# Another order of all engines' instructions, and operand slots turned per outward layer, in windowed attention with two gated layers

## The chip, the cores and the metric

The kernel runs on one core of a Trainium2 chip. The metric is the device time of one execution in microseconds (us), taken as the median of three runs. The engines are TensorE (PE in the rows, PEld its weight loads), VectorE (DVE), ScalarE (ACT), GpSimd (POOL) and SyncE (SP), which issues every transfer here.

## The reference

```python
# q, k, v: batch 4, heads 8, sequence 576, head size 64
scores = scale * np.matmul(q, k.transpose(0, 1, 3, 2))
mask = (rel >= 0) & (rel < window)                    # window 128
scores = np.where(mask, scores + bias[None], -1000000000.0)
attn = np.exp(scores - np.max(scores, axis=-1, keepdims=True))
attn = attn / (np.sum(attn, axis=-1, keepdims=True) + 1e-09)
x = np.matmul(attn, v)                                # -> 2304 tokens x 512
# layer 0 and layer 1, each with w_in 512 x 2048 and w_out 2048 x 512
h = x @ w_in
g = h * np.tanh(sp)                                   # layer 0, sp = softplus(h)
g = np.where(h > 0.0, h, alpha * (np.exp(np.minimum(h, 0.0)) - 1.0))   # layer 1
x = g @ w_out
```

## The kernel before

The work has five parts that follow one another. Attention runs over 4 batches, 4 head pairs and 3 row blocks each (function `unit`: scores in tile `ps_s`, a transpose in `ps_t`, values in `ps_o`, the result in `xc`). The inward product of layer 0 (`hidden`, products at L914 into `hA`, `hB`, `hC`) runs batch by batch beside the attention of the batch behind it. The outward product of layer 0 (`outward`, products at L1001 into `oA`, `oB`, `oC`), the inward product of layer 1 and the outward product of layer 1 follow, in three column chunks each. Every product of the two layers is done with seven block products instead of eight (steps P1, P5, P6, P2, P7, P3, P4). Every operand is split into two parts, a rounded copy at L529 (ACT, or L530 on DVE) and the remainder by a subtraction at L534 (DVE or POOL); three of the four part products are kept. So one step on one operand tile is six products in `hidden`, and 12 in `outward`, which I call a group. There are 56 groups in a batch of `hidden` in layer 0, and 28 in a chunk of `outward`, 84 in a layer.

Four weight sets (w = 0 to 3) arrive as 64-bit numbers in tiles `raw` and are turned into floats in `convert`: two ACT steps (L593 and L597, a few of the second on DVE), a shift on DVE (L601), an add at L604 that may stand on POOL or on DVE, and sums of blocks. Sets 1 to 3 go to DRAM and come back as tiles `w` (`load_weights`). The gate of layer 0 is the function Mish on ACT (L978), applied when the tiles `graw` are read back for the outward product; it needs another function table than the rest. So ACT loads a table when it goes from Mish to the conversions at L593 and back.

The order is made ahead by the class `Plan`. Each operation has a priority worked out backwards from due times (`rank_all`), with a shift for its group from the table `SHIFT`. `order` then plays the program through with assumed costs and emits the instructions in the order found; where an operation may stand on two engines, it chooses there. Engines run their instructions strictly in the order emitted. While PE has nothing ready in the first 90 us of that play, `order` emits unused products (L489) into it; I call them fills. No product of the kernel is placed before the time `WARM`.

On-chip tiles lie in rings of slots. A tile takes the next slot of its ring and waits until the tile before it in that slot has been read. The outward operand `hl` has its own: of the first step of layer 0, and of two steps at its end, in ring `L0`; of the first step of layer 1 in ring `L1`; all others in ring `L`, which has five slots.

```python
    wide_s, right_s = slots(wide, "w", 6, 4 * T2), slots(right, "r", 7, 4 * T2)
    plan.ring("L0", right_s[4:])
    plan.ring("L", right_s[4:] + wide_s[4:])
    plan.ring("L1", wide_s[4:])
```

The ring `L` goes on counting from layer 0 into layer 1.

Of the kernel before, what the change touches and what calls it, by code (L numbers as in the profile page):

```python
# [11 lines left out]
F32R = mybir.dt.float32r  # L12
# [9 lines left out]
AT = dict(copy=2.27, both0=-0.71, both1=-8.32, both2=-3.61, turn=0.99, held=10.7, fill=90, enough=1.5, norma=-0.5, normp=2.42,  # L22
          kappa=1.29, lag=0.9, first=-64.52, unit=2.69, h1=50.67, chunk=70.1, lead=30.24, dt=1.35, dma=-14.73,
          conv=-27.63, wadd=-0.1, soft0=0, soft1=0, soft2=0, soft3=0, eq=4, ep=2, et=6, er=3, eb=0, eraw=3, side0=1,
          side1=2, depth=4, ahead=7.48, hb=5)
SHIFT = {
# [77 lines left out]
class Plan:  # L104
# [3 lines left out]
    WARM = 6.9  # L108
# [253 lines left out]
def mm_cost(n):  # L362
    return 0.000417 * n + (0.0125 if n < 384 else 0.0153)
# [795 lines left out]
```

## Time and profile before

| | |
|---|---|
| median of 3 runs | 868.72 us (867.3 to 870.11) |
| the profiled execution: time, span | 868.03 us, 866.3 us |
| PE busy | 843.4 us, 97% of the span |
| DVE, ACT, POOL busy | 723.1, 628.3, 132.4 us |
| chain that ended last | PE 70%, DVE 12%, ACT 11%, DMA 3%, issue 3% |
| DMA | 187.67 MB, mean 217 GB/s |

The span runs from the first to the last instruction. In a row of the time line the number in brackets is how long the engine stood idle before the instruction, and who ended that. Each product group lasts some 2.1 us, so an idle time of 1 us on PE is half a group.

### The profile page before, as it was taken

The numbers are of one execution on the slowest core, as the hardware profiler recorded it, in microseconds if no ns is written. First come the engines' busy times: TensorE is split into PE (matmuls) and PEld (weight loads), VectorE is DVE, ScalarE is ACT, GpSimd is POOL, SyncE is SP. The second block draws the span as 40 slices with busy tenths as digits, with TensorE's granted clock in tenths as the row PEclk, the third lists the DMA queues.
The fourth block names the chain that finished last, engine by engine and source line by source line (L and its number), as shares of the span: only waits on it lengthen the run. The fifth ranks groups of instructions, "written<-read, shape, count | busy, mean of one in ns | idle before, by whom it ended". The sixth has DMA issues, their size and how long they took to land.

```text
span 866.3 us, 15682 instructions
## 1 busy us (share of the span) xinstructions
PE 843.4 (97%) x5403; PEld 794.1 (92%) x5403; DVE 723.1 (83%) x1590; ACT 628.3 (73%) x1421; POOL 132.4 (15%) x115
## 2 busy tenths in 40 slices
PE   9988999999999999899899999999999999999998
PEld 6767788898889999899899999989999999999998
DVE  8999998778877689799889988895978988877863
ACT  6989997677767688875897868976998944333442
POOL 0434120000003000135213043121300000000000
PEclk9999999999999999999999999999999999999999
DMA  7436667877867886674677778676778957226102
GB/s 277 138 119 214 190 211 244 280 267 258 253 225 246 286 290 235 233 254 149 232 264 258 254 249 284 218 266 214 261 253 275 313 182 229 105 96 229 41 1 73
DMA packets 85967, 187.67 MB, mean 217 GB/s; under 512 B 8576, under 2 KB 30080, under 8 KB 85888
## 3 DMA queue, kind: packets, MB, share of 16 engines
q1 hardware_dynamic: 85888, 186.68, 64.2%
q8 instruction: 42, 0.69, 0.3%
q14 instruction: 37, 0.30, 0.1%
HBM read 117.44 MB, written 69.21 MB: 215 GB/s over the span
## 4 chain that ended last, share of the span: by engine, by line
PE 70%; DVE 12%; ACT 11%; DMA 3%; issue 3%; POOL 0%; SPq 0%; DVEq 0%; ACTq 0%; POOLq 0%
PE oA L1001 19%; PE hA L914 16%; PE oC L1001 11%; PE hC L914 8%; PE hB L914 4%; PE oB L1001 4%; PE ps_o L828 3%; DMA raw<-in_w_dram 2%; PE ps_s L725 2%; DVE hl L534 2%; PE ps_t L780 2%; DVE graw L534 1%; ACT hl L529 1%; ACT p L745 1%; ACT p L760 1%
## 5 line engine op out<-in xcount | busy, mean ns | idle before, releaser
L914 PE MATMUL hA<-xt,w 128*128 128x288 f32 (+1 forms) x1344 | 232.9, 319 | 2.3 <-ACT g L529 1.7
L529 ACT ACTIVATE hl<-graw 128x768 fp32r<-128x768 f32 x161 | 134.9, 843 | 128.1 <-PE oA L1001 63.8
L1001 PE MATMUL oA<-hl,w 128*128 128x384 f32 x1152 | 215.2, 338 | 4.2 <-DVE hl L534 2.4
L914 PEld LDWEIGHTS hA<-xt,w 128*128 128x128 f32 x1344 | 209.4, 189 | 8.0 <-ACT g L529 3.7
L534 DVE TENSOR_TENSOR hl<-graw,hl 128x768 fp32r<-128x768 f32 x168 | 165.8, 996 | 52.7 <-ACT hl L529 52.3
L1001 PEld LDWEIGHTS oA<-hl,w 128*128 128x128 f32 x1152 | 202.6, 188 | 7.0 <-DVE hl L534 4.8
L914 PE MATMUL hC<-xt,w 128*128 128x288 f32 (+1 forms) x672 | 119.7, 317 | 0.2 <-DVE g L897 0.2
L1001 PE MATMUL oC<-hl,w 128*128 128x384 f32 x576 | 111.0, 343 | 4.3 <-DVE hl L534 2.4
L1001 PEld LDWEIGHTS oC<-hl,w 128*128 128x128 f32 x576 | 103.0, 190 | 6.7 <-DVE hl L534 4.1
L914 PEld LDWEIGHTS hC<-xt,w 128*128 128x128 f32 x672 | 104.6, 188 | 3.0 <-issue 1.0
L534 DVE TENSOR_TENSOR graw<-graw 128x768 f32<-128x768 f32 x96 | 92.7, 977 | 4.2 <-ACT graw L978 1.8
L604 POOL TENSOR_TENSOR bits<-bits,raw 128x512 int32<-128x512 int32 x34 | 56.1, 1655 | 254.0 <-DVE bits L601 134.7
L529 ACT ACTIVATE g<-hA 128x288 f32<-128x288 f32 (+1 forms) x144 | 61.0, 434 | 26.6 <-PE hA L914 25.3
L745 ACT ACTIVATE p<-p,st 128x128 f32<-128x128 f32 x144 | 56.4, 396 | 13.8 <-DVE st L741 13.3
L534 DVE TENSOR_TENSOR w<-w 128x512 fp32r<-128x512 f32 x84 | 59.3, 730 | 6.2 <-ACT w L529 5.6
L914 PE MATMUL hB<-xt,w 128*128 128x288 f32 (+1 forms) x336 | 60.5, 317 | 2.4 <-DVE g L897 2.1
L914 PEld LDWEIGHTS hB<-xt,w 128*128 128x128 f32 x336 | 52.5, 188 | 4.2 <-DVE g L897 2.4
L1001 PE MATMUL oB<-hl,w 128*128 128x384 f32 x288 | 54.3, 338 | 0.0
L1001 PEld LDWEIGHTS oB<-hl,w 128*128 128x128 f32 x288 | 50.9, 188 | 0.2 <-DVE hl L534 0.2
L529 ACT ACTIVATE w<-w 128x512 fp32r<-128x512 f32 x83 | 49.3, 625 | 1.2 <-DMA w<-w_in 1.0
L896 ACT ACTIVATE e<-e 128x384 f32<-128x384 f32 x96 | 49.1, 529 | 0.7
L593 ACT ACTIVATE raw<-raw 128x512 f32<-128x512 f32 x64 | 43.0, 675 | 8.0 <-DMA raw<-in_w_dram 7.5
(100 smaller groups left out, 1109.2 us busy)
## 6 DMA issues: line engine op xcount, KB each, us to landing
graw<-gate SPq DMA_DIRECT2D x96, 384.0 KB, 4.6
raw<-in_w_dram SPq DMA_DIRECT2D x64, 512.0 KB, 5.3
gate<-g SPq DMA_DIRECT2D x64, 288.0 KB, 3.6
gate<-g SPq DMA_DIRECT2D x48, 384.0 KB, 3.9
w<-w_out SPq DMA_DIRECT2D x56, 256.0 KB, 4.0
qkv<-in_qkv_dram SPq DMA_DIRECT2D x16, 512.0 KB, 4.9
w_out<-bits SPq DMA_DIRECT2D x32, 256.0 KB, 5.1
w<-w_in SPq DMA_DIRECT2D x28, 256.0 KB, 3.7
```

Source lines behind the costliest of these rows:

```text
L529: ways = [("act", act_cost(n, sbuf), lambda: nc.scalar.activation(o(), i(), AF.Copy), 0.0), ("dve", dve_cost(n, sbuf), lambda: nc.vector.t ...
L534: emit = lambda eng: eng.tensor_tensor(out=o(), in0=x(), in1=y(), op=op)
L593: act(DM, lambda raw=raw: nc.scalar.activation(raw()[:, :, 1].bitcast(F32), raw()[:, :, 1].bitcast(F32), AF.Prelu, scale=2.0 ** -112, alph ...
L604: add = lambda eng, raw=raw, bits=bits: eng.tensor_tensor(out=bits().bitcast(I32), in0=bits().bitcast(I32), in1=raw()[:, :, 0].bitcast(I32 ...
L725: nc.tensor.matmul(pss[j]()[:, n, w0:2 * P], qs()[rs, n * P:(n + 1) * P], ks()[rs, ko + w0:ko + 2 * P], start=n == 0, stop=True, skip_grou ...
L745: act(P, lambda n=n, j=j: nc.scalar.activation(prob()[:, n, j], prob()[:, n, j], AF.Exp, scale=-1.0, bias=st()[:, 0, n, j:j + 1], accum_ou ...
L760: ("act", act_cost(P, True, 1), lambda y=y, f=f: nc.scalar.activation(y(), y(), AF.Copy, scale=f()), AT["norma"]),
L780: nc.tensor.transpose(ps()[:, j], prob()[:, n, j], ident)
L828: nc.tensor.matmul(o()[j * D:(j + 1) * D, c0:c0 + math.prod(y.shape[1:])], vn()[:kr, n, j], y, start=n == 0, stop=n == nkb - 1, skip_group ...
L896: act(T, lambda: nc.scalar.activation(e(), e(), AF.Relu, scale=-1.0, bias=1.0), (), [e], due)
L914: nc.tensor.matmul(ps(), w()[:, a, wi, cs], x()[:, b, k], start=step in FIRST and k == 0 and m == 0, stop=k == 1 and m == 2, skip_group_ch ...
L1001: nc.tensor.matmul(bk[name, d](), w()[:, a, wi, cs], x()[:, b, k], start=step in FIRST and f + k == 0 and m == 0, stop=f + k == NQ - 1 and ...
```

## The change

The diff touches only what sets the order, the choice between engines, and the slots; the arithmetic is the same. The table `SHIFT` is replaced. `Plan` assumes a higher transfer rate (400 instead of 270 GB/s) with a surcharge of 1.4 on the loads of `raw` and of one kind of `qkv`, slightly higher costs on every engine, and lets products of the kernel start at 4.0 us of its play instead of 6.9. A penalty for DVE work that shares a port with a busy POOL is raised (`held`), a table switch on ACT gets a negative penalty (`turn`), and transfers are held back more (`ahead`). The ring `L` is split: layer 0 uses `La` in the order w4, w5, r5, r6, r4, layer 1 uses `Lb`, which is that order turned by two.

```diff
-AT = dict(copy=2.27, both0=-0.71, both1=-8.32, both2=-3.61, turn=0.99, held=10.7, fill=90, enough=1.5, norma=-0.5, normp=2.42,
-          kappa=1.29, lag=0.9, first=-64.52, unit=2.69, h1=50.67, chunk=70.1, lead=30.24, dt=1.35, dma=-14.73,
...
-          side1=2, depth=4, ahead=7.48, hb=5)
+AT = dict(copy=2.27, both0=-0.71, both1=-8.32, both2=-3.61, turn=-3.27318, held=58.562, fill=90, enough=1.5, norma=-0.5,
+          normp=2.42, kappa=1.30746, lag=0.862655, first=-64.52, unit=2.69, h1=50.67, chunk=70.1, lead=30.24, dt=1.35,
+          dma=-7.42452, conv=-27.63, wadd=-0.1, soft0=0, soft1=0, soft2=0, soft3=0, eq=4, ep=2, et=6, er=3, eb=0,
+          eraw=3, side0=1, side1=2, depth=4, ahead=-51.5873, hb=5, lrot=2)
 SHIFT = {
-    "H000P1": -7.2, "H001P1": 4.9, "H001P6": 13.2, "H002P4": -0.5, "H002P6": -1.8, "H003P7": 0.4, "H003d": 11.8,
...
+    "H000P1": -11, "H000P2": -4.1, "H000P3": -8.6, "H000P4": -3.4, "H000P5": -16.2, "H000P6": -42, "H000P7": -9.8,
...
-    LATENCY = dict(pe=0.2, act=0.16, dve=0.13, pool=0.1, sp=0.0)
+    LATENCY = dict(pe=0.25, act=0.21, dve=0.18, pool=0.15, sp=0.05)
...
-    WARM = 6.9
+    WARM = 4.0
...
-    RATE, OUTSTANDING, LANDING = 270e3, 8, 1.9
+    RATE, OUTSTANDING, LANDING = 400e3, 8, 1.95
...
-    return 0.000417 * n + (0.0125 if n < 384 else 0.0153)
+    return 0.000417 * n + (0.013 if n < 384 else 0.0158)
...
-    return 0.000833 * n + 0.052 + 0.041 * sbuf + 0.093 * extra
+    return 0.000833 * n + 0.059 + 0.041 * sbuf + 0.093 * extra
...
-    return (0.00052 if fast else 0.001042) * n + 0.068 + 0.062 * extra
+    return (0.00052 if fast else 0.001042) * n + 0.075 + 0.062 * extra
...
-    plan.ring("L", right_s[4:] + wide_s[4:])
+    ls, lr = wide_s[4:] + right_s[5:] + right_s[4:5], int(AT["lrot"])
+    plan.ring("La", ls)
+    plan.ring("Lb", ls[lr:] + ls[:lr])
...
-                (), [(raw, 0), (raw, 1)], due)
+                (), [(raw, 0), (raw, 1)], due, 1.4)
...
-                     ("dve", 0.16 + 0.00104 * DM, lambda add=add: add(nc.vector), AT["wadd"])],
+                     ("dve", 0.07 + 0.00104 * DM, lambda add=add: add(nc.vector), AT["wadd"])],
...
-                [have[x][1] for x in which.split()], [("wsd", w, q, x) for x in which.split()], due, 1.2)
+                [have[x][1] for x in which.split()], [("wsd", w, q, x) for x in which.split()], due)
...
-        dma(P * cut[3] * 4, lambda: nc.sync.dma_start(out=t(), in_=src), (), [t], t0 - 10)
+        dma(P * cut[3] * 4, lambda: nc.sync.dma_start(out=t(), in_=src), (), [t], t0 - 10, 1.4 if part == 1 else 1.0)
...
-                x = buf("L0" if at_end else "L1" if layer and ci == 0 and i == 0 else "L", (2, 2, T), F32R, "hl")
+                x = buf("L0" if at_end else "L1" if layer and ci == 0 and i == 0 else ("La", "Lb")[layer], (2, 2, T), F32R, "hl")
```

Line numbers move by 40 from L529 on (L1001 becomes L1041, L914 becomes L954, L529 becomes L569). Three places show what the order has become.

On PE, at the passage from the inward to the outward product of layer 0, there stands before:

```order
L914 MATMUL hC<-xt,w 128x288 x6
L1001 MATMUL oA<-hl,w 128x384 x12
L914 MATMUL hA<-xt,w 128x288 x6
L1001 MATMUL oA<-hl,w 128x384 x36
L1001 MATMUL oC<-hl,w 128x384 x24
```

and now:

```order
L954 MATMUL hA<-xt,w 128x288 x6
L1041 MATMUL oA<-hl,w 128x384 x12
L954 MATMUL hA<-xt,w 128x288 x6
L1041 MATMUL oA<-hl,w 128x384 x24
L1041 MATMUL oC<-hl,w 128x384 x12
L1041 MATMUL oA<-hl,w 128x384 x12
L1041 MATMUL oC<-hl,w 128x384 x24
```

The first group of step P5 (`oC`) stood behind all four groups of step P1 (`oA`) and stands now ahead of the fourth of them.

On ACT, at the first passage to the conversions' table in that outward product (`raw` are the conversions, `graw` is Mish, `hl` the rounded copy of the operand), there stands before:

```order
L593 ACT_TABLE_LOAD
L593 ACTIVATE raw<-raw 128x512
L597 ACTIVATE raw<-raw 128x512
L529 ACTIVATE hl<-graw 128x768
L593 ACTIVATE raw<-raw 128x512
L597 ACTIVATE raw<-raw 128x512
L978 ACT_TABLE_LOAD
L978 ACTIVATE graw<-graw 128x768
L529 ACTIVATE hl<-graw 128x768
```

and now:

```order
L633 ACT_TABLE_LOAD
L633 ACTIVATE raw<-raw 128x512
L637 ACTIVATE raw<-raw 128x512
L569 ACTIVATE hl<-graw 128x768
L569 ACTIVATE y<-oC 128x384
L633 ACTIVATE raw<-raw 128x512
L637 ACTIVATE raw<-raw 128x512
L569 ACTIVATE hl<-graw 128x768 x3
L569 ACTIVATE y<-oA 128x384 x2
L569 ACTIVATE hl<-graw 128x768 x3
L1018 ACT_TABLE_LOAD
L1018 ACTIVATE graw<-graw 128x768 x2
```

Six copies of `hl` stand now between the conversions and the load back to Mish, where there was none. Over the whole outward product ACT loads a table 12 times instead of 10.

On DVE, in the inward product of layer 1 where its last operand `x` is combined (`e` and `g` belong to the gate, `sums` and `bits` to the conversions), there stands before:

```order
L897 SCALAR_TENSOR_TENSOR g<-hA,e 128x384
L534 TENSOR_TENSOR sums<-bits 128x256
L601 TENSOR_SCALAR bits<-raw 128x512
L534 TENSOR_TENSOR sums<-sums,bits 128x256
L534 TENSOR_TENSOR x_7181<-x_7181 128x2x384
L897 SCALAR_TENSOR_TENSOR g<-hA,e 128x384
```

and now:

```order
L937 SCALAR_TENSOR_TENSOR g<-hC,e 128x384
L937 SCALAR_TENSOR_TENSOR g<-g,e 128x384
L574 TENSOR_TENSOR x_7249<-x_7249 128x2x384
L574 TENSOR_TENSOR g<-hA,g 128x384
L937 SCALAR_TENSOR_TENSOR g<-hA,e 128x384
L574 TENSOR_TENSOR hB<-hB,g 128x384
```

The conversions no longer stand around it. Of the 64 halves of weight blocks that are converted, 16 stood on DVE behind the start of this part and 6 stand there now; of the adds at L604 POOL had 13 there and has 2. Over the whole kernel POOL has 22 of these adds instead of 34, and DVE 42 instead of 30. PE has 139 fills instead of 155, 15 instead of 29 of them ahead of the first scores.

## Rows read from the trace of the kernel before

**Rows 1.** Stretches: start:end, length, then busy (instructions) of PE, PEld, DVE, ACT, POOL; clock.

```profile
0.00:44.60 44.60, 42.95 (x373) 31.38 (x373) 39.75 (x205) 37.41 (x136) 10.32 (x18) 1.00 0.60 208
44.60:92.00 47.40, 41.63 (x313) 33.54 (x309) 45.09 (x159) 40.93 (x134) 16.16 (x14) 1.00 0.49 165
92.00:310.00 218.00, 217.34 (x1693) 195.09 (x1693) 177.75 (x592) 166.98 (x497) 22.95 (x19) 1.00 0.76 249
310.00:500.00 190.00, 183.62 (x1024) 180.79 (x1023) 171.06 (x207) 151.66 (x219) 41.64 (x30) 0.99 0.71 240
500.00:686.00 186.00, 182.85 (x1026) 180.91 (x1025) 156.49 (x274) 156.95 (x339) 41.31 (x34) 0.99 0.77 255
686.00:723.00 37.00, 34.98 (x191) 33.13 (x192) 34.34 (x44) 20.02 (x30) 0.00 (x0) 1.00 0.61 217
```

**Rows 2.** Groups of instructions: count, busy us, mean ns, idle before them.

```profile
L489 PE MATMUL unused<-const-bfloat16-1.0 128*128 128x256 bf16 x145 | 21.4, 292 | 0.8 <-PEq L1149 0.8
...
L604 DVE CUSTOM_DVE_ANT_0 bits<-raw,bits 128x1024 uint16<-128x1024 uint16 x30 | 20.5, 684 | 0.8 <-ACT raw L597 0.3
...
L593 ACT ACT_TABLE_LOAD x5 | 6.4, 1283 | 0.4 <-DMA raw<-in_w_dram 0.3
...
L534 DVE TENSOR_TENSOR graw<-graw 128x768 f32<-128x768 f32 x96 | 92.7, 977 | 4.2 <-ACT graw L978 1.8 <-DMA graw<-gate 1.5
```

**Rows 3.** Time line of PE in layer 0's inward part: start, length, instructions, [idle before].

```profile
5.93 0.93 PE L725 MATMUL ps_s<-qkv 64*128 64x128 f32 x8
...
117.08 0.80 PE L914 MATMUL hA<-xt,w 128*128 128x288 f32 x4 [0.24 <-DVE w L534]
```

**Rows 4.** Time line of PE in layer 0's outward part, where it waited.

```profile
320.42 0.44 PE L1001 MATMUL oC<-hl,w 128*128 128x384 f32 x1 [0.93 <-ACT hl L529]
321.42 5.85 PE L1001 MATMUL oC<-hl,w 128*128 128x384 f32 x23 [0.56 <-DVE hl L534]
355.75 0.44 PE L1001 MATMUL oC<-hl,w 128*128 128x384 f32 x1 [1.00 <-ACT hl L529]
357.44 2.21 PE L1001 MATMUL oC<-hl,w 128*128 128x384 f32 x11 [1.25 <-DVE hl L534]
424.77 0.44 PE L1001 MATMUL oA<-hl,w 128*128 128x384 f32 x1 [1.76 <-ACT hl L529]
425.76 2.18 PE L1001 MATMUL oA<-hl,w 128*128 128x384 f32 x11 [0.55 <-DVE hl L534]
```

**Rows 5.** Time line of ACT and DVE at the first of these waits.

```profile
319.53 0.84 ACT L529 ACTIVATE hl<-graw 128x768 fp32r<-128x768 f32 x1 [0.36 <-PE oA L1001]
...
320.40 0.96 DVE L534 TENSOR_TENSOR hl<-graw,hl 128x768 fp32r<-128x768 f32 x1 [0.59 <-ACT hl L529]
```

**Rows 6.** Stretches as in rows 1, of 3.4 us, behind two of PE's waits.

```profile
322.06:325.48 3.42, 3.42 (x12) 3.42 (x12) 3.42 (x5) 3.25 (x5) 0.00 (x0) 0.50 1.03 394
325.48:328.89 3.41, 3.41 (x21) 3.41 (x21) 3.38 (x5) 2.10 (x3) 0.00 (x0) 1.00 1.05 406
...
583.65:587.07 3.42, 3.42 (x14) 3.42 (x15) 2.01 (x5) 1.51 (x3) 0.00 (x0) 0.69 0.81 266
587.07:590.48 3.41, 3.41 (x18) 3.41 (x17) 1.30 (x3) 2.12 (x5) 0.00 (x0) 0.82 0.58 202
```

**Rows 7.** Time line of POOL, DVE and PE in layer 1's inward part.

```profile
580.80 1.47 POOL L604 TENSOR_TENSOR bits<-bits,raw 128x512 int32<-128x512 int32 x1
581.05 2.04 DVE L534 TENSOR_TENSOR x<-x 128x768 f32<-128x768 f32 x1
...
583.61 1.32 PE L914 MATMUL hB<-xt,w 128*128 128x384 f32 x6 [2.09 <-DVE g L897]
```

**Rows 8.** Time line of PE at the start of layer 1's outward part, where it waited.

```profile
686.50 4.60 PE L1001 MATMUL oA<-hl,w 128*128 128x384 f32 x23 [0.60 <-DVE hl L534]
...
705.45 2.20 PE L1001 MATMUL oA<-hl,w 128*128 128x384 f32 x11 [1.04 <-DVE hl L534]
```

More of the change, by code (lines that the diff above doesn't have):

```diff
@@ L20 @@
 GROUPS = ((0, 256, 0, 256), (256, 256, 128, 384), (512, 64, 384, 192))
-AT = dict(copy=2.27, both0=-0.71, both1=-8.32, both2=-3.61, turn=0.99, held=10.7, fill=90, enough=1.5, norma=-0.5, normp=2.42,
-          kappa=1.29, lag=0.9, first=-64.52, unit=2.69, h1=50.67, chunk=70.1, lead=30.24, dt=1.35, dma=-14.73,
-          conv=-27.63, wadd=-0.1, soft0=0, soft1=0, soft2=0, soft3=0, eq=4, ep=2, et=6, er=3, eb=0, eraw=3, side0=1,
-          side1=2, depth=4, ahead=7.48, hb=5)
+AT = dict(copy=2.27, both0=-0.71, both1=-8.32, both2=-3.61, turn=-3.27318, held=58.562, fill=90, enough=1.5, norma=-0.5,
+          normp=2.42, kappa=1.30746, lag=0.862655, first=-64.52, unit=2.69, h1=50.67, chunk=70.1, lead=30.24, dt=1.35,
+          dma=-7.42452, conv=-27.63, wadd=-0.1, soft0=0, soft1=0, soft2=0, soft3=0, eq=4, ep=2, et=6, er=3, eb=0,
+          eraw=3, side0=1, side1=2, depth=4, ahead=-51.5873, hb=5, lrot=2)
 SHIFT = {
[55 rows of a table removed]
[93 rows of a table added]
 class Slot:
```

146 rows, old and new, of the table SHIFT are left out of this document.

## The prediction, made before the changed kernel ran

> **What bounds the kernel now.** I read first the busy time by stretches, cut at the borders of the parts. PE is idle 1.65 us of the first 44.6, 5.77 of the next 47.4, 0.66 of the 218 up to 310, then 6.38, 3.15 and 2.02 us in the outward part of layer 0, the inward part of layer 1 and the start of its outward part [rows 1]; after 723 us it waits only for the last output (3.3 us of the span). So PE is the bound, and an order can win only these waits, the fills that stand where PE would wait, and time at the lower clock. The fills are 145 into the spare bank, 21.4 us busy or 0.148 us each [rows 2], and ten more.
>
> Second, what ended each wait. In layer 0's outward part it is each time `hl`, on ACT or DVE [rows 4]. The first shows why: ACT's copy at 319.53 had waited for PE [rows 5]. The first tile of step P5 takes slot r4 of ring `L`, which the last tile of P1 held, and PE has both next to each other. So copy (0.84), subtraction (0.96) and product stand in a row, and nothing covers them. A group of 12 products lasts 2.15 us (183.62 us for 1024 [rows 1]). By ring and order of PE, ten of the layer's 84 tiles have fewer than two groups between the last read of their slot and their own use, and this one has none; copy and subtraction alone take 1.8 us, so one group covers them only if both engines stand ready. Third, the granted clock. After the first wait one stretch of 3.42 us ran at 0.50, the lower of the two levels (1.2 and 2.4 GHz), with 12 products where the next at 1.00 has 21; PE had been idle 1.49 us just before. After the wait of 2.09 us at 583.61 two stretches show 14 and 18 [rows 4, 6, 7]. That costs 9/21 of 3.41 = 1.5 us and 10/21 = 1.6 us. Fourth, that wait of 2.09: DVE's subtraction on `x` took 2.04 us, a like one of 768 columns takes 0.98 on average, and POOL's add ran from 580.80 to 582.27 beside it [rows 2, 7]. PE waited for a gate step queued behind it on DVE.
>
> **The change part by part.** My sum is made against the profiled execution, 868.03 us, which lies 0.7 us under the median of 868.72.
>
> Start and first inward part. With 15 instead of 29 fills ahead, the first scores can start before 5.93 [rows 3]. The earliest `qkv` may let them start up to 1.6 us sooner, but the second block's data comes no sooner, so I count at most a fraction. Sixteen fills fewer are 16 x 0.148 = 2.4 us, worth that only where data let products come forward. Ahead of the operands of the 28th group of the first batch stand eight exponentials and eight normalizations fewer on ACT, and eight scores fewer on DVE: attention of the next batch is held back. They are paid later: ahead of the 56th group both kernels have the same attention, and DVE has three more adds (3 x 0.684 = 2.1 us [rows 2]). DVE is 45.09 of 47.40 us busy in this stretch [rows 1], and as late as 117.08 PE waited for a weight that DVE had just made [rows 3]. So the upper end is 2.4 + 5.77 = 8.2 us, the lower end nothing, if DVE stays the bound (that it turns into a loss is a rival below). I take half, 4 us. What hides the rest up to 310 us is that PE has no gap there; it stays so unless transfers come late.
>
> Layer 0's outward part. The new ring starts with w4 and w5, not with the slot just in use, and the first group of P5 now stands ahead of the fourth of P1. Counted the same way, no tile of the layer has fewer than two groups of cover (4.2 us). The wait of 1.49 us and its 1.5 us of clock should go. The second, 2.25 us at 355 to 357 [rows 4], came where conversions, two table loads and Mish stood between copies of `hl`; there six copies now stand between the conversions and the load back, and the tiles are made early. I count it gone: 1.49 + 1.5 + 2.25 = 5.2 us. The third place, 1.76 + 0.55 us at 425 [rows 4], is the pile load, conversion, load back, Mish; the new order has that pile twice within three copies of `hl`, with five slots as before. I leave its 2.3 us as it is. The bounds are 0 and 7.5 us.
>
> The Trainium skill, on the page ScalarE: Activation LUTs, section Rules for kernel authors, advises to group functions by table set and to do all of one set before switching. The change goes the other way, from 10 loads to 12; by the loads' duration in the rows this would take 2.6 us off the gain if all of it lay on the path.
>
> Inward part of layer 1. Its conversions go from 16 to 6 and POOL's adds from 13 to 2. The wait of 2.09 us and its 1.6 us of clock go with the collision: 3.7 us. The remaining 1.06 us of idle time [rows 1] I leave. Bounds 0 and 4.8 us. The ten conversions moved forward land mostly in the stretch up to 310 us, where DVE is 177.75 of 218 us busy [rows 1] and PE does not wait; that cover is gone only if DVE falls behind there.
>
> Start of layer 1's outward part. PE is idle 2.02 us [rows 1], of which 0.60 and 1.04 are the two longest waits for `hl` on DVE [rows 8]. Nine of the first 28 tiles had one group of cover, now two. DVE is 34.34 of 37 us busy there [rows 1], so a part may stay; I count 1.6 us, bounds 0 and 2.0.
>
> Sum of what is named: 4 + 5.2 + 3.7 + 1.6 = 14.5 us.
>
> New waits. The order was worked out with assumed durations, and the old order shows how far such a plan misses: behind 92 us, up to 723, PE is idle 0.66 + 6.38 + 3.15 + 2.02 = 12.2 us [rows 1], plus 3.1 us of clock. The new order rests on the same kind of plan at other places, which the order view cannot show. I charge a third of the 15.3, since the thin covers are gone, so 5 us; bounds 0 and 15.3. Net 9.5 us.
>
> **The rivals.** First, more than that: the named waits go and hardly any comes, -14.5 to -17 us, some 852 us. For it speak the doubled covers, against it that DVE is nearly full in two stretches.
>
> Second, ACT's piles decide in layer 0's outward part. Against two piles, each with two loads of 1.283 us [rows 2], five slots give no more lead than before; the second pile costs another wait like the first (2.3 us) and a stretch of lower clock (1.5 us) at each of the two. That takes 2.3 + 3.0 = 5.3 us off: 9.5 - 5.3 = 4.2, some 864 us.
>
> The rule of the Trainium skill on grouping table sets (ScalarE: Activation LUTs, Rules for kernel authors) points the same way; no run here has yet priced it.
>
> Third, the waits only move. Where PE waits less, its next operands are due sooner; PE then waits as much elsewhere, and the sum of new waits is that of the old, 15.3 instead of 5. Then 14.5 - 15.3 leaves +0.8, no change, 868 us.
>
> Fourth, slower: DVE becomes the bound. Twelve adds come to it from POOL, 12 x 0.684 = 8.2 us [rows 2]. It is 95% busy from 44.6 to 92 us and 93% at the start of layer 1's outward part [rows 1]. If all of them fall where DVE sets the pace, the first term's 4 us is lost and 8.2 us come on top: -9.5 + 4 + 8.2 = +2.7, some 871 us. It decides from the point where DVE's share between 92 and 310 us, now 82%, passes about 95%, since then the moved work has no gap to fall into. Against it: POOL's work also stretches DVE's [rows 7], and less of it runs.
>
> **How the numbers follow.** The forecast, 868.03 - 9.5 = 858.5 us, has a chance of 0.42. The first rival has 0.18, the second 0.18, the third 0.10, the fourth 0.12. No change means within 0.3%, 2.6 us, which is about what a measurement of this kernel can tell. Faster then holds the forecast and the first two rivals, 0.78; same 0.10; slower 0.12. The range leaves out the slower case, a bit of the third, and gains beyond 20 us: 848 to 868 us.
>
> **What would show it.** In the changed profile: at layer 0's outward part no copy of `hl` on ACT that waits for the group just ahead, and no stretch at 0.50 at its entry; idle time of PE there near 2.5 us and not 6.38. In the inward part of layer 1 POOL nearly idle and no subtraction of `x` near 2 us. Idle time of PE under 5 us between 44.6 and 92 us, and the last product of the first batch some 4 us sooner. The forecast is wrong if PE's idle time behind 92 us stays near 12 us at other places, if DVE's share passes 95% over long stretches, or if the clock falls at more places than two.

## The result: 0.5 to 0.6% slower, and the profile after

The changed kernel takes 873.58 us (median of 6 runs, 870.62 to 876.43), the kernel before, run beside it, 868.92 us. The medians lie 0.54% apart; the ratio, which is not formed from the medians, is 1.0061, with a 95% interval of 1.0035 to 1.0087. I had forecast 858.5 us and left nothing above 868 in the range.

The profiled execution of after has a span of 871.6 us, 5.3 us more than before. The table by stretches has the borders of [rows 1], so the two can be read line by line (start:end, length, then busy time and instructions of PE, PEld, DVE, ACT, POOL; granted clock, DMA share, GB/s):

```profile
0.00:44.60 44.60, 43.12 (x357) 31.18 (x358) 38.76 (x212) 36.44 (x135) 9.93 (x18) 1.00 0.55 192
44.60:92.00 47.40, 45.18 (x346) 37.50 (x344) 46.79 (x160) 43.99 (x139) 18.92 (x16) 1.00 0.56 187
92.00:310.00 218.00, 209.38 (x1624) 186.45 (x1621) 186.48 (x614) 170.99 (x501) 27.54 (x26) 1.00 0.83 284
310.00:500.00 190.00, 179.57 (x995) 174.17 (x993) 158.33 (x198) 145.53 (x207) 49.95 (x36) 0.98 0.68 231
500.00:686.00 186.00, 184.41 (x1043) 182.93 (x1044) 147.35 (x257) 148.98 (x317) 13.62 (x13) 1.00 0.61 208
686.00:723.00 37.00, 37.00 (x211) 36.69 (x210) 36.01 (x49) 25.74 (x43) 0.00 (x0) 1.00 0.68 248
723.00:871.60 148.60, 145.06 (x825) 144.67 (x823) 107.44 (x131) 52.89 (x70) 0.00 (x0) 0.99 0.32 112
```

Length less PE's busy time is PE's idle time. It went from 1.65 to 1.48, from 5.77 to 2.22, from 0.66 to 8.62, from 6.38 to 10.43, from 3.15 to 1.59, from 2.02 to 0.00 and from 3.3 to 3.54 us. So four stretches did better. Two lost more than all of that: the stretch from 92 to 310 us, where PE had never waited, lost 8.0 us, and layer 0's outward part 4.1 us. The sum of the seven differences is +5.0 us, nearly the whole of the 5.3. In the chain that ended last, transfers (DMA) make up 12% of the span, where they made up 3%:

```profile
PE 61%; DVE 13%; DMA 12%; ACT 10%; issue 3%; POOL 1%; SPq 0%; DVEq 0%; ACTq 0%; POOLq 0%
```

Where the loss arises can be read at the first product of layer 0's outward part. Up to it both orders have done the same products of attention and of the inward part, all but the last group. Before and after:

```profile
310.07 2.28 PE L1001 MATMUL oA<-hl,w 128*128 128x384 f32 x12
...
315.74 2.29 PE L1041 MATMUL oA<-hl,w 128*128 128x384 f32 x12
```

The new order is 5.7 us late there, and from there to the end both take the same, 555.9 and 556.2 us: what the outward part loses, the parts behind it give back.

**Where PE waits between 92 and 316 us.** First what PE waited for, in the new order (engine, tile, line, waited for: us in total, times, longest); in the old one two waits of 0.2 and 0.3 us are all there is. Then what ACT waited for where it was a transfer, in the new order, and last in the old one:

```profile
PE hB L954 <- ACT g L569: 3.0, 3, 2.0
PE hA L954 <- ACT g L569: 1.9, 3, 0.9
PE hA L954 <- DVE w L574: 1.1, 1, 1.1
PE ps_s L765 <- DMA qkv<-in_qkv_dram: 1.0, 3, 0.4
PE hA L954 <- DVE g L574: 1.0, 2, 0.5
...
ACT w L569 <- DMA w<-w_out: 6.0, 9, 1.3
ACT raw L633 <- DMA raw<-in_w_dram: 5.6, 6, 1.7
ACT raw L637 <- DMA raw<-in_w_dram: 4.3, 3, 1.7
ACT g L569 <- DMA gate<-g: 3.3, 2, 3.0
```

```profile
ACT raw L593 <- DMA raw<-in_w_dram: 3.2, 2, 1.7
ACT g L529 <- DMA gate<-g: 1.0, 1, 1.0
```

ACT stood 19.2 us on transfers, where it was 4.2 us. PE's largest item is `g` on ACT, the copy that frees a bank of the inward product. One place shows how the two hang together, ACT and then PE:

```profile
282.79 0.68 ACT L633 ACTIVATE raw<-raw 128x512 f32<-128x512 f32 x1 [2.34 <-DVE w L574]
283.36 0.67 ACT L637 ACTIVATE raw<-raw 128x512 int32<-128x512 uint32 x1
284.05 1.28 ACT L1018 ACT_TABLE_LOAD   x1
285.35 0.84 ACT L1018 ACTIVATE graw<-graw 128x768 f32<-128x768 f32 x1
286.09 0.69 ACT L569 ACTIVATE g<-hA 128x288 f32<-128x288 f32 x2
...
286.84 1.06 PE L954 MATMUL hB<-xt,w 128*128 128x288 f32 x6 [2.03 <-ACT g L569]
```

ACT stands 2.34 us before a conversion. The row names DVE, whose work on `w` happened to end then, but `raw` is filled by a transfer that was issued at 275.65; transfers of this kind took up to 7.0 us to land there. Behind the conversion stand a table load and Mish, and behind these the copies of `g` that PE needs. PE is 2.03 us idle. The six waits for `g` on ACT (4.9 us in all) each have such a wait of ACT for a transfer in the 4.1 us before them, and 1.0 us are waits for `qkv` itself. The 1.15 us for `w` at 123.18 are another case: DVE's subtraction on `w` took 1.77 us there, beside a step of 1.49 us on POOL, where the other six of its form take 0.7 us on average; that is the collision of [rows 7] at another place.

The transfers themselves are hardly slower: a weight block issued from 92 to 310 us lands after 5.4 us in the median and 7.3 at most, in the old kernel after 5.3 and 8.3. They are late for the place at which the new order has them used.

**The wait at 434 us.** In layer 0's outward part, ACT, PE, and the stretches of 3.4 us in which PE starts again:

```profile
426.44 0.83 ACT L569 ACTIVATE hl<-graw 128x768 fp32r<-128x768 f32 x1
427.29 1.28 ACT L633 ACT_TABLE_LOAD   x1
428.58 0.68 ACT L633 ACTIVATE raw<-raw 128x512 f32<-128x512 f32 x1
429.26 1.28 ACT L1018 ACT_TABLE_LOAD   x1
430.56 0.84 ACT L1018 ACTIVATE graw<-graw 128x768 f32<-128x768 f32 x1
431.31 0.64 ACT L637 ACTIVATE raw<-raw 128x512 int32<-128x512 uint32 x1
431.85 0.83 ACT L569 ACTIVATE hl<-graw 128x768 fp32r<-128x768 f32 x1
...
434.28 0.66 PE L1041 MATMUL oA<-hl,w 128*128 128x384 f32 x1 [4.34 <-ACT hl L569]
...
433.45:436.86 3.41, 2.33 (x6) 1.96 (x7) 3.37 (x6) 1.48 (x3) 0.00 (x0) 0.50 0.61 171
436.86:440.28 3.42, 3.42 (x13) 3.42 (x13) 3.39 (x6) 2.27 (x3) 1.36 (x1) 0.56 0.99 361
```

Two copies of `hl` on ACT stand 5.4 us apart (426.44 and 431.85), and between them are the pile of load, conversion, load, Mish and a second conversion step. Another such pile ended at 424.2. PE waited for the next copy, at 433.31. It stood 4.34 us, and then went for two stretches at or near the lower clock (0.50 and 0.56).

### The profile page after: what moved, and what is told of

It reads as the page before. It is cut to its first block, busy times and chain, and to the rows that moved or that the text cites. A ratio compares the mean times of both kernels' runs of the same rounds, so it can differ in the third digit from the quotient of the medians.

```text
span 871.6 us, 15673 instructions
## 1 busy us (share of the span) xinstructions
PE 843.7 (97%) x5387; PEld 793.6 (91%) x5387; DVE 721.2 (83%) x1616; ACT 624.6 (72%) x1403; POOL 120.0 (14%) x109
## 4 chain that ended last, share of the span: by engine, by line
PE 61%; DVE 13%; DMA 12%; ACT 10%; issue 3%; POOL 1%; SPq 0%; DVEq 0%; ACTq 0%; POOLq 0%
PE hA L954 16%; PE oA L1041 14%; PE hC L954 8%; PE oC L1041 7%; DMA raw<-in_w_dram 5%; PE hB L954 4%; PE oB L1041 3%; DVE hl L574 3%; PE ps_o L868 2%; DMA qkv<-in_qkv_dram 2%; DVE graw L574 2%; PE ps_s L765 2%; ACT hl L569 2%; DVE w L574 2%; PE ps_t L820 1%
## 5 line engine op out<-in xcount | busy, mean ns | idle before, releaser
L954 PE MATMUL hA<-xt,w 128*128 128x288 f32 (+1 forms) x1344 | 232.9, 318 | 5.8 <-ACT g L569 2.1
L1041 PE MATMUL oA<-hl,w 128*128 128x384 f32 x1152 | 217.1, 340 | 5.6 <-ACT hl L569 4.3
L954 PEld LDWEIGHTS hA<-xt,w 128*128 128x128 f32 x1344 | 207.8, 188 | 13.0 <-ACT g L569 4.2
L569 ACT ACTIVATE hl<-graw 128x768 fp32r<-128x768 f32 x158 | 131.6, 843 | 112.2 <-PE oA L1041 42.0
L1041 PEld LDWEIGHTS oA<-hl,w 128*128 128x128 f32 x1152 | 204.3, 189 | 8.4 <-ACT hl L569 4.6
L954 PE MATMUL hC<-xt,w 128*128 128x288 f32 (+1 forms) x672 | 119.3, 316 | 1.0 <-DVE xt L574 0.6
L1041 PE MATMUL oC<-hl,w 128*128 128x384 f32 x576 | 109.8, 340 | 3.9 <-DVE hl L574 3.0
L954 PEld LDWEIGHTS hC<-xt,w 128*128 128x128 f32 x672 | 104.4, 188 | 4.5 <-issue 1.4
L1041 PEld LDWEIGHTS oC<-hl,w 128*128 128x128 f32 x576 | 102.2, 189 | 5.7 <-DVE hl L574 4.5
L569 ACT ACTIVATE g<-hA 128x288 f32<-128x288 f32 (+1 forms) x143 | 61.1, 435 | 16.9 <-PE hA L954 12.9
L644 POOL TENSOR_TENSOR bits<-bits,raw 128x512 int32<-128x512 int32 x22 | 35.9, 1637 | 224.5 <-DVE bits L641 94.5
L954 PE MATMUL hB<-xt,w 128*128 128x288 f32 (+1 forms) x336 | 60.9, 318 | 3.0 <-ACT g L569 3.0
L569 ACT ACTIVATE w<-w 128x512 fp32r<-128x512 f32 x81 | 49.7, 631 | 12.2 <-DMA w<-w_out 6.9
L954 PEld LDWEIGHTS hB<-xt,w 128*128 128x128 f32 x336 | 52.6, 188 | 4.8 <-ACT g L569 4.2
L1041 PE MATMUL oB<-hl,w 128*128 128x384 f32 x288 | 54.0, 338 | 0.0
L1041 PEld LDWEIGHTS oB<-hl,w 128*128 128x128 f32 x288 | 50.8, 188 | 0.3 <-DVE hl L574 0.3
```

Source lines behind the costliest of these rows:

```text
L569: ways = [("act", act_cost(n, sbuf), lambda: nc.scalar.activation(o(), i(), AF.Copy), 0.0), ("dve", dve_cost(n, sbuf), lambda: nc.vector.t ...
L644: add = lambda eng, raw=raw, bits=bits: eng.tensor_tensor(out=bits().bitcast(I32), in0=bits().bitcast(I32), in1=raw()[:, :, 0].bitcast(I32 ...
L954: nc.tensor.matmul(ps(), w()[:, a, wi, cs], x()[:, b, k], start=step in FIRST and k == 0 and m == 0, stop=k == 1 and m == 2, skip_group_ch ...
L1041: nc.tensor.matmul(bk[name, d](), w()[:, a, wi, cs], x()[:, b, k], start=step in FIRST and f + k == 0 and m == 0, stop=f + k == NQ - 1 and ...
```

## The experiments

Most of them play a recorded order: a list SEQ of all steps in order, each with its engine, and the fills, takes the place of what the planner would find. With the list of either kernel this gives that kernel instruction for instruction. The diff of all of these is

```diff
-    for emit in plan.order():
+    for emit in replay(plan, SEQ):
         emit()
```

and a list is then put together from the two, or changed at single steps. Ratios are to the kernel before on the same chip and differ a little from those of the medians. Beside e1 to e4 its median was 869.41 us, beside e5 to e8 868.73 and beside e9 to e11 868.22, so a difference of two runs of different groups is uncertain by about 1 us.

### Which stretch loses: two orders joined

e3_new_h0_old_rest: SEQ is the first 2280 steps of the new order and then what is left in the old one, with the old ring.

> The new order up to the end of layer 0's inward part (some 2280 of the 4228 steps), then what is left in the old order with the old ring; no conversion is then left in layer 0's outward part. Theory of late data: the 5 us won up to 92 us and the 8 us lost from there to 316 us both stay, PE's idle time between 92 and 316 us near 8.6 us as in the new order; behind that the old waits at conversions (2.25 and 2.3 us) have no conversion left and go: 868.9 + 4 - 4.5 = about 868 us. Rival, that the inward part is sound and the loss lies only in what follows: PE idle there under 3 us and about 860 us.

Measured: 865.49 us, 0.9956 (0.9938 to 0.9975). The loss up to 310 us stayed where it was, the outward part behind it lost next to nothing:

```profile
92.00:310.00 218.00, 208.83 (x1607) 184.86 (x1606) 185.61 (x612) 169.80 (x498) 27.20 (x26) 1.00 0.83 282
310.00:500.00 190.00, 188.51 (x1081) 187.57 (x1080) 157.71 (x199) 134.40 (x196) 13.41 (x10) 1.00 0.59 200
```

PE is idle 9.17 us and then 1.49 us; the 1.49 are the old wait at the entry (0.93 + 0.56). With 4 weight loads in the outward part instead of 12 its other waits are gone. The first product of the outward part starts at 315.85 us, as late as in the changed kernel, and still the run ends ahead of both: what the blocks converted early cost is won back, and more, where they no longer stand. I had put the time 2.5 us too high.

e6_new_start: the same with the first 1500 steps, up to some 185 us.

> The new order for its first 1500 steps (105 of the 224 product groups of layer 0's inward part, up to some 185 us), then what is left in the old order. In the new order's trace the balance at equal work stands at -4 to -5 us there. Theory (gain at the start, loss by late data behind): the gain stays and nothing is lost later, 864 to 865 us, PE idle from 92 to 316 us clearly under 8 us. Rival, that the start only borrows work which is paid later, with DVE as the bound: 868 to 869 us.

Measured: 865.26 us, 0.9964 (0.9943 to 0.9984), the time expected. The stretch from 92 to 310 us, cut at 193 us, in this run, and then the second half in the changed kernel (the old kernel has 0.66 us of idle time in the whole stretch [rows 1]):

```profile
92.00:193.00 101.00, 95.97 (x747) 82.32 (x745) 89.10 (x321) 79.53 (x255) 13.74 (x14) 1.00 0.76 253
193.00:310.00 117.00, 116.97 (x906) 108.53 (x907) 87.06 (x262) 83.68 (x233) 8.10 (x6) 1.00 0.74 240
```

```profile
193.00:310.00 117.00, 111.93 (x859) 102.18 (x858) 96.43 (x290) 90.67 (x249) 13.41 (x12) 1.00 0.89 308
```

Up to 193 us, most of it still in the new order, PE has gaps of 5.0 us. Where the old one has taken over there are none (0.03 us). The new order has 5.1 us there, with 0.89 of DMA share and 308 GB/s. So the new order behind the 1500th step is what loses.

That the new start wins is not shown by this trace. Up to 310 us PE is idle 1.05 + 2.33 + 5.06 = 8.4 us here and 8.1 us in the old kernel, and the first product of the outward part stands nearly where it stood (310.07 in the old kernel):

```profile
309.45 2.28 PE L1001 MATMUL oA<-hl,w 128*128 128x384 f32 x12
```

In e9, with the same start, it stands at 310.68, and in the four other profiled runs of the old start (e2, e5, e8, e10) between 309.32 and 309.93. What the start wins is given back before 310 us. Of the 3.4 us between the two spans 2.8 come behind this product, where both run the same list; there the old kernel's trace has two places at a lower clock [rows 6] and this one has none. Why the median of seven runs is 3.5 us lower all the same stays open.

### Are late transfers the cause, or DVE?

e4_more_after and e5_more_before: both orders as they are, with one more transfer behind each of 48 weight loads (in the old kernel the same lines). The texts below say 56 and 14.7 MB; the traces have 48 and 12.6 MB.

```diff
-            dma(P * DM * 8, lambda raw=raw, s=s: nc.sync.dma_start(out=raw().rearrange("p n w -> p (n w)"), in_=s),
+            dma(P * DM * 8, lambda raw=raw, s=s, f=f, w=w: (nc.sync.dma_start(out=raw().rearrange("p n w -> p (n w)"), in_=s),
+                w and nc.sync.dma_start(out=dummy[w * NF + f], in_=s[:, :512])),
```

> The new order with one more transfer of 256 KB, from memory to memory and read by nobody, behind each of the 56 loads of weight blocks that come after the first inward ones (14.7 MB more on 187.7 MB). Theory of late data: the new order has no slack to transfers, so each later landing makes ACT and then PE wait: 880 us or more, while the old order (run apart) moves by 2 us at most. Rival, DVE with 12 more adds as the cause: the transfers don't matter and the time stays within 2 us of 873.6.

> The old order with the same extra transfers as the run before of the new one (256 KB from memory to memory behind each of the 56 later weight loads). Theory of late data: the old order was made for slower transfers and holds its data back, so it moves by 3 us at most, 872 us or less, where the new one lost 20 us (893.6). Rival, that any order loses about as much to the traffic: 885 us or more.

Measured: the new order 893.58 us (1.0291, interval 1.0261 to 1.032), the old one 873.09 us (1.0046, 1.0028 to 1.0063). So the same traffic costs the new order 20.0 us and the old one 4.4, 1.4 more than I had allowed. ACT's waits for weight loads and PE's for `qkv` from 92 to 316 us, in the new order (its lines are one higher) and then in the old one:

```profile
PE ps_s L766 <- DMA qkv<-in_qkv_dram: 6.8, 5, 1.9
...
ACT raw L634 <- DMA raw<-in_w_dram: 13.8, 10, 2.6
```

```profile
PE ps_s L726 <- DMA qkv<-in_qkv_dram: 0.8, 1, 0.8
...
ACT raw L594 <- DMA raw<-in_w_dram: 3.5, 4, 1.4
```

The load on the DMA engines alone doesn't make the loss. With the extra transfers the old order has as high a share from 92 to 310 us as the new one without them (0.83), and PE is idle 1.1 us, not 8.6:

```profile
92.00:310.00 218.00, 216.91 (x1692) 194.92 (x1691) 177.01 (x590) 167.38 (x495) 22.81 (x19) 1.00 0.84 273
```

e7_adds_pool_after: the new order with 16 adds at L644 that DVE does in the inward part given back to POOL, in the same places of the list.

```diff
 L641 TENSOR_SCALAR bits<-raw 128x512
 L574 TENSOR_TENSOR sums<-bits 128x256
-L644 ISA bits<-raw,bits 128x1024
 L574 TENSOR_TENSOR w<-bits,w 128x512
```

> The new order with 16 of its adds of weight bits in layer 0's inward part given from DVE back to POOL, as in the old kernel, at the same places. Rival of the prediction, DVE as the bound: DVE loses 16 x 0.69 = 11 us of work there and the time falls, to 866 us or less. Theory of late data: the waits stay, and the add of 1.3 to 1.6 us on POOL only lengthens the conversions: 873 to 877 us.

Measured: 879.77 us (1.0133, 1.0114 to 1.0153), slower than the changed kernel and above both ranges. DVE has less to do and PE waits no less, so DVE's share was not the bound. Its busy time from 92 to 310 us fell from 186.48 of 218 us to

```profile
92.00:310.00 218.00, 208.19 (x1595) 184.46 (x1594) 181.07 (x595) 169.16 (x496) 45.44 (x39) 0.99 0.82 279
```

and PE's idle time rose from 8.62 to 9.81 us. Up to 316 us the adds on DVE fall by 9.6 us, its busy time only by 5.4 up to 310, so the test is weaker than planned. That the longer add in a conversion is what costs is argued, not shown: the first product of the outward part is 2.3 us later than in the changed kernel, the span 6.9 us longer, and the rest comes in later parts, where no run asks the cause.

### What the table loads cost

e1_noload_after and e2_noload_before: both orders as they are, with

```diff
-                raw()[:, :, 1].bitcast(F32), raw()[:, :, 1].bitcast(F32), AF.Prelu, scale=2.0 ** -112, alpha=-2.0 ** 32),
+                raw()[:, :, 1].bitcast(F32), raw()[:, :, 1].bitcast(F32), AF.Copy if w else AF.Prelu, scale=2.0 ** -112, **({} if w else dict(alpha=-2.0 ** 32))),
```

> The new order, instruction for instruction, but in the conversions of all weights except the first inward ones ACT's Prelu is a Copy, which needs no other table than Mish (the converted weights are then not the right ones; the times of all instructions stay). The two loads of 1.283 us around each conversion in layer 0's outward part go. Theory of the loads: the wait of PE for ACT's hl at 434 us (4.34 us), its stretch at the lower clock (about 1.7 us) and the waits at 385 and 421 us go, so 873.6 - 7 = about 866 to 867 us. Rival, late data (ACT stands there because the conversion's own transfer lands late): the wait of 4.34 us stays above 3 us and the time within 2 us of 873.6.

> The same edit in the old order. Theory of the loads: the waits at 355 us (2.25 us) and 425 us (2.3 us) go, the one at 320 us stays with its 1.5 us of clock, since no conversion stands there: 868.9 - 4.5 = about 864 us. Rival: the waits come from the slots and copies in a row, and the loads only add a little: above 867 us.

Measured: the new order 866.97 us (0.9965, 0.9946 to 0.9983) and so 6.6 us less than the changed kernel; the old order 862.11 us (0.9915, 0.9891 to 0.9938), 7.3 us less, where I had expected 4.5 (the waits at 355 and 425 us are gone as expected, and this execution has no stretch at a lower clock either). In the new order no wait of 4 us is left; the longest in layer 0's outward part is

```profile
436.70 0.44 PE L1041 MATMUL oA<-hl,w 128*128 128x384 f32 x1 [1.65 <-ACT hl L569]
```

and ahead of it ACT had waited 1.59 us for a `graw`, a transfer again. Without its loads the old order is 4.9 us ahead of the new one, so the loads are not the cause of the difference between the two orders.

The Trainium skill, page ScalarE: Activation LUTs, section Rules for kernel authors, advises to group functions by table set. The runs agree: 10 and 12 loads of 1.28 us lie on ACT, and without them both orders are about 7 us shorter.

e11_told_after: the planner of the changed kernel counts no load for Prelu; here it is told.

```diff
-                (), [(raw, 1)], due)
+                (), [(raw, 1)], due, table="exp")
```

> The changed kernel whose planner is told that Prelu needs the table of Exp (before, it counts no load for it); the table of shifts and all costs stay, so the order moves where conversions stand among Mish. Theory of the loads: the plan gives the pile at 420 to 434 us more lead, the wait of 4.34 us falls to 2 us or less, and the time by 3 to 6 us, to about 868 to 870 us; the 8.6 us of idle time between 92 and 316 us stay. Rival, that the order as fitted is the better one in spite of the wrong cost: 873 us or more.

Measured: 867.26 us (0.9987, 0.9969 to 1.0005), 6.3 us less than the changed kernel and a little better than expected, and in the two stretches

```profile
92.00:310.00 218.00, 208.30 (x1605) 184.88 (x1606) 185.63 (x612) 169.72 (x498) 26.97 (x26) 1.00 0.84 283
310.00:500.00 190.00, 186.55 (x1064) 184.03 (x1062) 176.78 (x221) 154.62 (x218) 49.51 (x35) 1.00 0.73 246
```

PE's idle time from 310 to 500 us fell from 10.43 to 3.45 us; that from 92 to 310 us stayed (9.70). The longest wait left in the outward part is 1.09 us. The load count went up, from 13 to 17 in the whole program. So it isn't the number of loads alone that counts; the lead that the order leaves for them fits, though the edit moves more of the order than that.

### Single terms, and a version that is faster than both

e8_h1_adds_dve: the old order with the 13 adds of POOL in layer 1's inward part done by DVE, in the same places; on POOL such rows go:

```diff
 L534 TENSOR_TENSOR sums<-bits,sums 128x256
-L604 TENSOR_TENSOR bits<-bits,raw 128x512 x2
 L534 TENSOR_TENSOR sums<-bits 128x256
```

> The old order with the 13 adds of weight bits that POOL does in layer 1's inward part given to DVE, at the same places. The prediction's third term (the collision of POOL's add with DVE's subtraction of x makes the wait of 2.09 us and 1.6 us at a lower clock): both go, 868.9 - 3.7 = about 865 us. Rival, that DVE's queue is what PE waits for and the added 13 x 0.69 = 9 us of DVE's work take the place of the collision: 868 to 871 us.

Measured: 866.19 us, 0.9975 (0.9962 to 0.9989). DVE's subtraction of `x` and PE behind it, to be read beside [rows 7]:

```profile
578.62 0.95 DVE L534 TENSOR_TENSOR x<-x 128x768 f32<-128x768 f32 x1
...
580.09 1.33 PE L914 MATMUL hB<-xt,w 128*128 128x384 f32 x6 [0.29 <-DVE g L897]
```

It takes 0.95 us instead of 2.04, and the wait is 0.29 us instead of 2.09, though DVE has nine more microseconds of adds. The collision with POOL was the cause.

e10_dve_sign_before: the old order, with the part of the conversion that needs the table put on DVE, in the 12 conversions of layer 0's outward part.

```diff
+            on_dve = w == 2 and q >= 2
...
+                if on_dve:
+                    f = x.bitcast(F32)
+                    nc.vector.scalar_tensor_tensor(out=f, in0=f, scalar=-2.0 ** 32, in1=f, op0=ALU.mult, op1=ALU.max)
+                nc.vector.tensor_scalar(out=bits(), in0=x, scalar1=3, scalar2=None, op0=ALU.logical_shift_left)
```

> The old order with only the sign step on DVE in those 12 conversions. With the loads gone the run with wrong weights gave 862.1; DVE's 12 more steps are 7 us of work, of which the gaps of 19 us of DVE in the outward part can take a part: 862 to 865 us. Rival, each step delays a subtraction of hl that PE waits for: 867 us or more.

e9_best: this, the new start of e6 and the adds of e8 in one list.

> Three pieces together: the new order for its first 1500 steps and the old one behind, the 13 adds of layer 1's inward part on DVE, and, in the 12 conversions that stand in layer 0's outward part, the sign step taken from ACT's Prelu to DVE (ACT scales with a Copy, DVE takes the larger of x and -2^32 x), so that no table is loaded between Mish and copies. If the three causes are separate, their gains add: -3.5 (new start), -2.5 (adds) and -7 (no loads, as in the old order with wrong weights) less what 12 more DVE steps of some 0.6 us cost in layer 0's outward part, where DVE is 171 of 190 us busy: 868.8 - 13 + 2 to 5 = 858 to 861 us. Rival, DVE takes the place of the loads: 863 us or more.

Measured: e10 865.08 us (0.9957, 0.9941 to 0.9972), at the upper end of what was expected; e9 862.40 us (0.9919, 0.99 to 0.9938), 1.4 us above it. That is 5.8 us less than before and some 11 us less than the changed kernel. Against the kernel before beside them, e10 alone has 3.1 us and e8 alone 2.5, together 5.7, so the new start adds next to nothing to them, as its traces say. DVE pays for the loads: a step takes 0.867 us, not 0.6, so 12 are 10.4 us, and DVE is 183.99 of 190 us busy in the outward part of e9. The row of e10:

```profile
L608 DVE SCALAR_TENSOR_TENSOR raw<-raw 128x512 f32<-128x512 f32 x12 | 10.4, 867 | 0.0
```

## Why the prediction was wrong, point by point

**Start: the signs came, the gain did not last.** I took 4 us. PE is idle 2.22 us from 44.6 to 92 us, under the 5 I had asked for, and the last product of the first batch ended 2.6 us sooner (125.8 against 128.4), not 4. But e6, which has nothing else of the new order, is idle as long as the old kernel up to 310 us (8.4 and 8.1 us) and starts the outward part at the same time. What I had said of the work (it is paid later) holds for the time too, and the third rival, that the waits only move, has the mechanism here. The medians of e6, 3.5 us lower, fit the number of the term; where these runs win it, no trace shows.

**Entry and first waits of layer 0's outward part: right.** At the entry PE has no gap, and of the 2.25 us at 355 one of 0.67 us is left, at 358 us. A new one of 0.89 + 0.55 us came at 385 us.

**The pile: the term was mis-sized.** I left 2.3 us as it was. It became 4.34 us with two stretches of low clock behind, and 1.13 us at 421. That is the second rival's mechanism: two piles within three copies of `hl`. I had read them in the order and given the case 0.18. e1 and e11 show the loads as the cause.

**Inward part of layer 1: right in mechanism.** The wait is gone, and POOL does nothing from 560 to 620 us. e8 finds 2.5 us for it, against 3.7 with the clock (see below).

**Start of layer 1's outward part: right, and larger.** All 2.02 us are gone, 1.6 were taken.

**New waits: the step that failed.** I took 5 us, a third of what the old order misses, up to 15.3 at most. Behind 92 us PE is idle 20.6 us up to 723, where the old order has 12.2 in all. Of the 12.2 I had counted 7.4 as gone, which leaves 4.8, so the new waits came to 15.8 us, three times the term and above its upper end; 8.0 of it came in the one stretch that I had left out of the sum. For that stretch I had said that PE has no gap "unless transfers come late", and named only DVE's share as the point from which the cover is gone. That is the premise that failed: eight of the ten conversions moved forward landed there, as I had said, and the cover went with DVE at 186.48 of 218 us (86%), far from the 95% I had set, because ACT stood 19.2 us on transfers instead of 4.2 with the copies for PE behind them. The rival of a slower kernel came near the time (871), but by luck, since its cause was the wrong one. What I didn't weigh stood in the diff: the planner assumes 400 instead of 270 GB/s. In the order too: 31 weight loads are issued from 92 to 310 us where there were 23. As I read it, an order that was found with slow transfers carries slack for them without anyone having put it there, and I took the misses of that order as the measure for the new one. e4 and e5 show the difference: the new order is between four and five times as sensitive to the same extra traffic. e3 and e6 show that the loss stays with the new order in that stretch, and e7 that it is not DVE's share.

**What stays open.** That the rate in the planner made the order tight is argued from the diff, not shown: the table of shifts was found together with it, and no run changes the one without the other. A run in which transfers get faster was not tried. Nor does a run tell apart two things that the new order does at once between 92 and 310 us: it converts eight weight blocks more there, and it puts them closer to their transfers. The runs with the loss have 30 or 31 weight loads there (after, e1, e3, e7, e11), those without have 23 (before, e6). Of the 0.62 + 0.62 us at 500 to 502 us, where PE waits for `xt`, no run asks the cause.

## What to carry to other kernels

An order fitted to assumed durations is as good as its slack for what the assumption leaves out (argued here from one pair of orders), and the misses of an older order say little of a newer one: look which assumed rate rose, and which in-order engine has an instruction behind a transfer. Before an engine's queue gets an instruction that may wait for data, ask what stands behind it; here a late weight block on ACT held the copies that free PE's banks. A cost that the planner doesn't know (a table load) turns into a wait at the place where the plan is tightest, and telling the planner was worth as much as taking the cost away. A wait that is gone is a gain only if a later product, behind the same work, starts sooner; here the first product of the next part showed that the gain of the start had been given back.

## What the runs showed of the hardware that I had not expected

The lower clock behind a wait comes in some executions and not in others. At the entry to layer 0's outward part, e6 has the first waits of [rows 4] to within a hundredth, and yet the stretch that answers to the first of [rows 6] runs at 1.00 with 21 products instead of 12:

```profile
319.81 0.44 PE L1001 MATMUL oC<-hl,w 128*128 128x384 f32 x1 [0.93 <-ACT hl L529]
320.80 4.33 PE L1001 MATMUL oC<-hl,w 128*128 128x384 f32 x23 [0.55 <-DVE hl L534]
...
322.00:325.41 3.41, 3.41 (x21) 3.41 (x20) 3.41 (x5) 2.70 (x4) 0.00 (x0) 1.00 1.03 397
```

In layer 1's inward part, e10 has a wait of 2.06 us and then a stretch at 0.57, e6 one of 2.07 us and no such stretch. Of the old kernel's 20 runs beside e9, five with a mean granted clock of 0.994 took 870.5 us on average and three with 1.000 took 867.9. So the 3.1 us of clock that I had counted as sure belong to chance in part; that fits with e8, which gives 2.5 us and not 3.7.
